# Attention into a softplus layer on one core: ten groups by seven block products instead of eight, a whole k cast with two half-size DMA transposes, 26 fillers, and a new written order

## The chip, the cores and the metric

The kernel runs on one core of one Trainium2 chip. A core has five engines with an instruction queue each: TensorE (PE) for matmuls, VectorE (DVE), ScalarE (ACT), GpSimd (POOL), and SyncE (SP), which here only issues DMAs. Every queue is worked off in order; semaphores make one engine wait for another. Matmuls write to PSUM, which has eight banks of 128 x 512 fp32; DVE and ACT can read PSUM. The metric is the device time of one execution in microseconds (us), lower is better.

## The reference, cut to what matters

```python
scores = scale * q @ k.T                       # 4 sequences, 8 heads, 768 tokens, head size 64
keep   = is_global | is_local                  # the first 8 tokens, and the last 96 up to the query
bias   = -slopes[h] * dist                     # dist = n_local for a global token outside the window
a      = softmax(where(keep, scores + bias, -1e9))
x      = (a @ v).reshape(3072, 512)            # heads side by side
h      = x @ w_in                              # 512 -> 2048
g      = maximum(h, 0) + log1p(exp(-abs(h)))   # softplus
out    = g @ w_out                             # 2048 -> 512, float32
```

Inputs and output are float32; the matmuls of the kernel are bf16.

## The kernel before, in words

The 3072 tokens are 24 blocks of 128. Two neighbouring blocks of a sequence make a unit (12 units, `UNITS`) and, in the order in which they are worked on, a group of 256 tokens (`NGRP` = 12) for the two big matmuls. Each block attends to itself and to the block before it, of which the first 8 keys, outside every window, are replaced by the 8 global ones.

For a unit, q, k and v are loaded as float32 (`load_unit`), cast to bf16 (`cast_q`, `cast_rows`) and q and k transposed, so that the head size lies on the partitions. For units 0 to 2 the transposes are matmuls (`transp_pe`); for units 3 to 11 they are DMA transposes issued from SP (`transp_dma`). `cast_rows` casts k and v in quarters of 64 x 512, because it also swaps halves of tokens between partitions; so a unit takes four k casts and then one transpose of 128 x 1024.

For a block n the steps have names that come back in the order below: `sc` scores (16 matmuls of 128 columns), `z` adds the bias from PSUM to SBUF (DVE), `ex` takes the exponential (ACT), `pv` multiplies by v (8 matmuls of 65 columns per half, the 65th gives the sum), `nm` divides (DVE), and `xt` transposes the result into XT: by matmuls for the first six blocks (with an eviction `xc`), by a DMA transpose from SP for the others. `gk` and `gv` copy the global keys and values. Blocks 0 and 1 get their bias by a matmul (`sb`).

For a group g: `a{g}.{p}` is one of eight pieces of the first matmul (8 matmuls of 256 columns, into one of the two banks h0 and h1), `e` takes its exponential and `ln` the logarithm of 1 + it, which is softplus (ACT). The second matmul is done in two ways. Groups 0 to 3 (`mm2`) take 2 x 16 matmuls of 512 columns into one bank per 128 tokens, then one copy `oc` and one store `st` each. Groups 4 to 11 (`FIRST_S` = 4) use a scheme in the manner of Strassen and Winograd on 2 x 2 blocks: five differences of token blocks (`token_sums`, named `ka`), seven products of eight 256-column matmuls each (`products`, named `b{g}.3`, `.4`, `.5`, `.2`, `.1`, `.7`, `.6`), and additions in the output buffer (`oe{g}.a` to `oe{g}.7`). The sums of weight blocks that this takes (`weight_sums`, 20 operations named `ws`) are made once.

What runs where and in what order is written out: `ORDER` is a list of all operations with the engine of each, in one sequence; each engine's queue is that sequence cut down to the engine. `Program` only checks that nothing stands before what it depends on. The numbers for durations and ranks in the code do nothing at run time. Which PSUM bank an operation uses is fixed by tables (`PE_KEYS`, `PV_KEYS`, `O_KEYS`, `S_KEYS`): from block 4 on `pv` uses the bank x, and products use the bank o except in the last two groups. 35 fillers (`fill`, matmuls on a blank tile into bank x) stand where the order leaves TensorE without work.

Loads of later units are held back by `gates`: each waits for a certain piece `a{g}.{p}` (`LEADS`).

Of the kernel before, what the change touches and what calls it, by code (L numbers as in the profile page):

```python
# [16 lines left out]
class Op:  # L17
    __slots__ = ("name", "eng", "fn", "deps", "sync", "ins")


class Program:


    def __init__(self, placed):
        self.placed = placed
        self.ops, self.writer, self.readers = {}, {}, {}

    def op(self, name, eng, dur, rank, fn, reads=(), writes=(), after=(), dma=None, sync=(), count=1,
           port=False, alts=None, mutex=None):
        o = Op()  # L30
        o.name, o.eng, o.fn, o.sync, o.ins = name, eng, fn, list(sync), None
        if alts:
            o.eng = self.placed[name]
            assert o.eng in alts, (name, o.eng)
            o.fn = lambda: fn(o.eng)
        assert o.eng == self.placed[name], name
# [19 lines left out]
    def in_order(self):  # L56

        done = set()
        for name in self.placed:
            o = self.ops[name]  # L60
            assert all(d.name in done for d in o.deps), (name, [d.name for d in o.deps if d.name not in done])
            done.add(name)
            yield o
        assert len(done) == len(self.ops)
# [4 lines left out]
blank:V ldq0.1:A iota:G ldk0.0:S fill0:P ldq0.0:A ldk0.1:S fill1:P dl0a:V fill2:P table:A ldq1.0:S dl1a:V dl0b:V  # L69
fill3:P dl0c:V ldv0:S fill4:P dl1c:V d0:G ldq1.1:S dl1e:V fill5:P d0e:V fill6:P ldk1.0:S biasTrue4:A biasTrue7:A  # L70
biasTrue0:V fill7:P biasFalse4:G biasTrue6:A biasTrue1:V castq0.1:A ldk1.1:S ones:G castk0.0:A biasFalse5:V ldv1:S
ident:G biasFalse7:A biasFalse2:V biasFalse1:A win0:S castq0.0:A castk0.1:G win1:S biasFalse0:V biasTrue3:A trq0.0:P
biasFalse6:A win3:S biasFalse3:A biasTrue5:A trk0.0:P biasTrue2:V cpq0.1:V fill8:P sb0.0:P cpk0.0:A cpq0.0:V fill9:P
castv0.00:G win2:S cpk0.1:A castq1.0:V castv0.11:A sc0.0:P castv0.01:V fill10:P ldq2.0:S sb1.0:P ex0.0:A castk1.0:G
sc1.0:P win4:S ex0.1:A sb1.1:P castq1.1:G win5:S ex1.0:A pv0.0:P sc1.1:P castv0.10:G nm0.0:V fill11:P fill12:P
ex1.1:A castk1.1:V pv0.1:P trq1.0:P castv1.10:G ldq2.1:S nm0.1:V fill13:P fill14:P cpq1.0:A castv1.11:V pv1.1:P
trk1.0:P nm1.1:V pv1.0:P cin0:G win6:S fill15:P cpk1.1:A cpk1.0:V fill16:P xt0:P cpq1.1:A fill17:P fill18:P
castv1.01:G xc0:A fill19:P win7:S fill20:P nm1.0:V sc2.0:P castv1.00:G cin1:A xt1:P z2.1:V fill21:P gk4:A fill22:P
cin3:G ldk2.0:S gv4.1:A fill23:P z2.0:V sc3.1:P fill24:P xc1:V gv4.0:G sc3.0:P ex2.0:A ldk2.1:S a0.1:P cin2:G z3.1:V
fill25:P a0.0:P e0.1:A z3.0:V castq2.0:G wout0:S ex2.1:A pv2.0:P a0.3:P e0.0:A nm2.0:V ln0.0:A fill26:P cin4:G  # L80
wout1:S fill27:P fill28:P pv2.1:P a0.2:P e0.3:A nm2.1:V ex3.1:A ldv2:S fill29:P cin5:V xt2:P castq2.1:G wout2:S
fill30:P ex3.0:A fill31:P xc2:V a0.5:P e0.2:A pv3.0:P cin6:G wout4:S fill32:P e0.5:A fill33:P nm3.0:V a0.4:P cin7:V
wout3:S pv3.1:P trq2.0:P e0.4:A castk2.0:G nm3.1:V a0.7:P ln0.1:A cpq2.0:V castk2.1:G xt3:P a0.6:P e0.7:A xc3:V
cpq2.1:A cout0:G trk2.0:P e0.6:A ldq3:S a1.1:P cpk2.0:V wout5:S ln0.2:A ws0.6:G wout6:S a1.0:P cpk2.1:V wout7:S
e1.1:A sc4.0:P ws0.4:G e1.0:A a1.3:P ln1.0:A z4.1:V cout1:G a1.2:P castv2.01:A z4.0:V ex4.1:A b1.0.0:P castv2.00:G
fill34:P b1.0.2:P gk5:A ws0.7:V e1.3:A b0.0.0:P b0.0.2:P ex4.0:A cout4:V sc5.0:P castv2.10:V a1.5:P e1.2:A cout3:G
z5.0:V cout2:A pv4.0:P a1.4:P ws0.1:G nm4.0:V ln0.3:A sc5.1:P b0.0.4:P e1.5:A castq3.0:G z5.1:V pv4.1:P castv2.11:A
b0.0.6:P b0.0.8:P cout5:A gv5.1:G ldk3:S nm4.1:V a1.7:P ws0.3:V ln1.1:A xt4:P b0.1.0:P ldv4:S ws2.6:V b0.0.10:P
trq3:S ex5.0:A cout6:V b0.1.2:P b0.1.4:P gv5.0:V e1.4:A b0.1.6:P xc4:V ex5.1:A b1.0.4:P ws2.1:V b0.1.8:P ws2.4:V
ln1.2:A pv5.0:P castk3.01:G b1.0.6:P nm5.0:V b0.1.10:P castk3.00:A a1.6:P castk3.10:V gk6:G ws2.3:V castk3.11:G  # L90
pv5.1:P b1.0.8:P e1.6:A nm5.1:V b0.0.12:P ldq4:S cout7:A b1.0.10:P ws1.3:V ws1.1:G trk3:S b0.1.12:P e1.7:A xt5:P
b0.0.14:P xc5:V b0.1.14:P ws2.7:V oc0.0.0:A a2.1:P ln1.3:A ws1.7:V a2.0:P ldk4:S e2.1:A ws1.4:V b1.0.12:P oc0.1.0:A
castq4.0:G b1.0.14:P ldv3:S e2.0:A a2.3:P ln2.0:A oc1.0.0:V gv8.0:G a2.2:P st1.0.0:S ws1.6:G e2.3:A ldq5:S gv8.1:A
# [59 lines left out]
LOAD_LEAD = 2.5  # L153
LEADS = {3: 2.25, 4: 2.75, 5: 3, 6: 3, 7: 3.5, 8: 3, 9: 3, 10: 3, 11: 2.75}
FILLERS = 35
TABLE_RANK = -9000.0
BIAS0_ON = ["ACT"]
BIASA_ON = ["ACT"]
PE_BIAS = (0, 1)
# [88 lines left out]
def kernel(  # L248
# [116 lines left out]
    def held(keys):  # L365

        return sorted({key[:2] for key in keys})
# [904 lines left out]
```

## Time and profile before

| | |
|---|---|
| time, median of 3 runs | 213.35 us (213.26 to 213.78) |
| span of the profiled execution | 213.6 us |
| PE busy | 202.9 us, 95% |
| ACT busy | 177.8 us, 83% |
| DVE busy | 158.3 us, 74% |
| POOL busy | 107.3 us, 50% |
| moved by DMA | 40.99 MB, mean 192 GB/s |

The profiled execution is one run of its own; its span, from the first to the last instruction, is 0.25 us above the median of the timed runs. Busy PE time is the union of matmuls whose ends are modelled, so overlapping matmuls count once and a busy PE may still be waiting for short moments. In the rows below, a group of instructions has its line, engine, operation, the tile written and the tiles read, shapes, count, busy time, the mean of one in ns, and the idle time of its engine just before. In the rows by stretches each engine has its busy us and, in brackets, its instructions. In the chain of work a row is a start, a duration and what ran.

### The profile page before, as it was taken

How to read it: one execution, taken by the hardware profiler on the slowest of the kernel's cores; microseconds unless marked ns; L12 is line 12 of the kernel's file. 1: busy time of each engine (PE TensorE's matmuls, PEld its weight loads, DVE VectorE, ACT ScalarE, POOL GpSimd, SP SyncE). 2: the span in 40 equal slices, each digit the busy share in tenths (PEclk: the TensorE clock that was granted, in tenths of full speed). 3: DMA queues.
4: the chain of work that ended last, by engine and by line, in shares of the span. 5: the costliest groups of instructions: out<-in, count | busy, mean ns of one | idle time of the engine just before them, and what ended most of it. 6: DMA issues, size and time to landing. Idle time of an engine off the chain costs nothing.

```text
span 213.6 us, 5384 instructions
## 1 busy us (share of the span) xinstructions
PE 202.9 (95%) x2149; PEld 159.8 (75%) x2163; DVE 158.3 (74%) x289; ACT 177.8 (83%) x257; POOL 107.3 (50%) x127
## 2 busy tenths in 40 slices
PE   6699999899999979999999999999999999999994
PEld 1465796556666557776898888988889889888883
DVE  6459577989585978667889869779879857535674
ACT  5787989988998679899998898888997998789410
POOL 4277495542887955751276764627544635003000
PEclk9799999999999999999999999999999999999999
DMA  5999999594999948999679791999759211500205
GB/s 199 326 363 387 387 354 354 203 221 120 302 197 290 147 112 187 274 227 237 198 192 182 193 227 13 186 233 204 183 126 245 77 25 42 142 19 2 98 13 188
DMA packets 69849, 40.99 MB, mean 192 GB/s; under 512 B 30144, under 2 KB 61376, under 8 KB 69824
## 3 DMA queue, kind: packets, MB, share of 16 engines
q1 hardware_dynamic: 69392, 39.99, 72.2%
q10 hardware_dynamic: 432, 0.66, 0.8%
q8 instruction: 17, 0.28, 0.5%
q14 instruction: 8, 0.07, 0.1%
HBM read 27.26 MB, written 6.29 MB: 157 GB/s over the span
## 4 chain that ended last, share of the span: by engine, by line
PE 81%; DVE 7%; issue 4%; ACT 3%; DMA 2%; POOL 1%; ACTq 0%; POOLq 0%; DVEq 0%
PE h_ps L956 37%; PE o_ps L512 18%; PE o_ps L1003 6%; PE s_ps L846 5%; PE x_ps L898 4%; PE s_ps L1003 3%; DMA raw<-in_q_dram 2%; PE x_ps L1116 2%; DVE z L872 2%; ACT e L971 2%; PE x_ps L512 1%; DVE vb L658 1%; PE s_ps L512 1%; PE s_ps L721 1%; DVE xs L910 1%
## 5 line engine op out<-in xcount | busy, mean ns | idle before, releaser
L956 PE MATMUL h_ps<-XT,w_in_bf 128*128 128x256 bf16 x768 | 94.5, 273 | 0.9 <-ACT e L971 0.9
L956 PEld LDWEIGHTS <-w_in_bf 128*128 128x128 bf16 x768 | 72.8, 98 | 12.6 <-issue 1.0
L971 ACT ACTIVATE e<-h_ps 128x512 f32<-128x512 f32 x96 | 59.1, 636 | 11.8 <-PE h_ps L956 11.1
L982 ACT ACTIVATE g<-e 128x1024 bf16<-128x1024 f32 x48 | 49.9, 1052 | 0.8
L872 DVE TENSOR_TENSOR z<-s_ps,biasA 128x1024 f32<-128x1024 f32 x38 | 45.8, 1219 | 5.4 <-PE s_ps L846 2.5
L879 ACT ACTIVATE pb<-z 128x1024 bf16<-128x1024 f32 (+1 forms) x44 | 43.2, 989 | 3.8 <-DVE z L872 3.5
L447 POOL TENSOR_TENSOR raw<-g 128x1024 bf16<-128x1024 bf16 x8 | 17.0, 2130 | 23.3 <-ACT g L982 17.7
L512 PEld LDWEIGHTS <-g 128*128 128x128 bf16 x256 | 24.6, 98 | 2.9
L1003 PE MATMUL o_ps<-w_out_bf,g 128*128 128x512 bf16 x87 | 22.5, 379 | 0.6 <-issue 0.2
L658 POOL CAST kb<-raw 64x512 bf16<-64x512 f32 x24 | 15.6, 652 | 14.1 <-DMA raw<-in_k_dram 9.0
L898 PEld LDWEIGHTS <-pb 128*128 128x128 bf16 x352 | 16.6, 98 | 5.0 <-issue 1.0
L512 PEld LDWEIGHTS <-raw 128*128 128x128 bf16 x192 | 18.4, 98 | 2.0
L1003 PEld LDWEIGHTS <-g 128*128 128x128 bf16 x128 | 11.5, 98 | 10.8
L658 POOL CAST vb<-raw 64x512 bf16<-64x512 f32 x24 | 15.5, 645 | 8.0 <-DMA raw<-in_v_dram 7.2
L909 DVE RECIPROCAL rcp<-x_ps 128x4 f32<-128x4 f32 x40 | 7.2, 180 | 14.8 <-PE x_ps L898 14.6
L910 DVE TENSOR_TENSOR xs<-x_ps,rcp 128x256 bf16<-128x256 f32 x40 | 17.0, 425 | 1.4
L764 POOL COPY vb<-vb 4x512 bf16<-4x512 bf16 x20 | 12.3, 616 | 11.2 <-PE x_ps L898 10.7
L512 PE MATMUL o_ps<-raw,raw 128*128 128x256 bf16 x144 | 17.8, 272 | 0.0
L634 POOL CAST qb<-raw 128x1024 bf16<-128x1024 f32 (+1 forms) x12 | 11.7, 972 | 10.5 <-DMA raw<-in_q_dram 10.4
L898 PE MATMUL x_ps<-vb,pb 128*128 128x65 bf16 x304 | 15.8, 193 | 0.8 <-DVE xs L910 0.8
L512 PE MATMUL o_ps<-raw,g 128*128 128x256 bf16 x128 | 15.9, 273 | 0.0
L447 POOL TENSOR_TENSOR g<-g 128x1024 bf16<-128x1024 bf16 x4 | 8.8, 2204 | 9.1 <-DVE raw L447 8.9
(110 smaller groups left out, 253.0 us busy)
## 6 DMA issues: line engine op xcount, KB each, us to landing
raw<-in_v_dram SPq DMA_DIRECT2D x12, 512.0 KB, 4.8
out_dram<-osb SPq DMA_DIRECT2D x22, 256.0 KB, 2.8
raw<-in_q_dram SPq DMA_DIRECT2D x9, 512.0 KB, 4.4
raw<-in_k_dram SPq DMA_DIRECT2D x9, 512.0 KB, 4.4
raw<-in_moe_w_in_dram SPq DMA_DIRECT2D x8, 512.0 KB, 9.5
raw<-in_moe_w_out_dram SPq DMA_DIRECT2D x8, 512.0 KB, 8.8
raw<-in_k_dram SPq DMA_DIRECT2D x6, 256.0 KB, 6.2
raw<-in_q_dram SPq DMA_DIRECT2D x4, 256.0 KB, 7.5
```

What stands on the lines that cost most here:

```text
L447: (nc.vector if eng == "DVE" else nc.gpsimd).tensor_tensor(dst, a[0], b[0], ALU.subtract)
L512: nc.tensor.matmul(psum(j), lhs[:, f // 2, f % 2, :], w(f), start=(f == 0), stop=(f == 7))
L658: copy_on[eng](dst, src)
L764: copy_on[eng](vb_of(prev)[sl, :, 0:D], vb_of(first)[sl, :, 0:D])
L872: nc.vector.tensor_tensor(z, src, bias, ALU.add)
L879: nc.scalar.activation(pb[:, 0:nr, :].rearrange("p (y a) b -> p y (a b)", y=2), src, AF.Exp, scale=1.0 / root_d)
L898: nc.tensor.matmul(xv[:, h, :], pb[:, 4 * (h % 2) + 2 * part + h // 2 if lone else u_all * (2 * (h % 2) + h // 2) + u, :], vb_of(prev if u ...
L910: nc.vector.tensor_tensor(xs[:, 4 * part : 4 * part + 4, :], xv[:, :, 0:D], rcp[:][:, :, None].to_broadcast([P, 4, D]), ALU.mult,)
L956: last = nc.tensor.matmul(hv[:, j, :], w_in_bf[:, m, fb * P : fb * P + P], XT[g % NXG][:, m, :], start=(m == 0), stop=(m == NM - 1),)
L971: nc.scalar.activation(e[:, p % 2, :, :].rearrange("p j (b t r) -> p (j b) r t", b=2, r=2), hb[:].rearrange("p (a r t) -> p a r t", a=4, r=2),
L982: nc.scalar.activation(gt[:, 2 * p - 2 : 2 * p + 2, :].rearrange("p a t -> p (a t)"), e[:].rearrange("p a j t -> p (a j t)"), AF.Ln, bias=1.0,
L1003: nc.tensor.matmul(bank(key)[:, 0 : z - a], gt[:, fb, ns * P : ns * P + P], w_out_bf[:, fb, a:z], start=(fb == 0), stop=(fb == NFB - 1),)
```

## The change

- `FIRST_S` goes from 4 to 2: groups 2 and 3 also take seven products. `mm2` stays for groups 0 and 1.
- For units 3 to 11, k is cast in one operation of 128 x 1024 (`castk{i}.0`) that regroups heads and token parity along the free dimension, and the swap between partitions that the four quarter casts did is done by the transposes: two DMA transposes of 64 partitions each (`trk{i}.0`, `trk{i}.1`), one per block, instead of one of 128.
- 26 fillers instead of 35.
- The PSUM bank of an operation is written beside it in `ORDER` (`pv0.1:P@h0`); `pv`, products and the early `xt` may now use x or o in turn.
- `ident` is made by a copy from a float32 identity.
- `ORDER` is new throughout: the sequence on every engine, and for many casts, copies and sums also the engine. The load order of the weights and of units 0 to 2 changes with it.

Operations by engine that change most (before, after): v casts on ACT 12, 19, on POOL 24, 16; k casts of units 3 to 11 on POOL 24, 6, on DVE 7, 1, on ACT 5, 2; token sums on DVE 28, 30, on POOL 12, 20; weight sums on DVE 10, 13, on POOL 10, 7; copies of global keys on ACT 10, 1, on POOL 2, 9; evictions of XT on ACT 1, 4, on DVE 5, 2; transposes of k on SP 9, 18.

```diff
-FIRST_S = 4
+FIRST_S = 2
-FILLERS = 35
+FILLERS = 26
...
+        if which == "k" and i not in WIDE:
+            into = tile_.rearrange("p (m r y d) -> p m r y d", m=NPAIR, r=2, y=2)
+            what = raw_t[slot][:].rearrange("p (m y r d) -> p m r y d", m=NPAIR, y=2, r=2)
+            op(f"castk{i}.0", "POOL", lambda eng: copy_on[eng](into, what), reads=raw_keys(slot),
+               writes=[("kb", i % NQB, z) for z in range(4)], port=True, alts=ANY)
+            return
...
-        op(f"tr{which}{i}", "SP", 1.45, rank, lambda: nc.sync.dma_start_transpose(dst, src), dma=(1.24, 18.0),
-           reads=[(which + "b", i % NQB, x) for x in range(4)], writes=keys)
+        for x in range(2):
+
+            def fn(x=x):
+                dst = kt_unit(i)[:, x, :, :].rearrange("p m (r t) -> p (m r) t", r=2)
+                return nc.sync.dma_start_transpose(dst, src[64 * x : 64 * x + 64].rearrange("p a h d -> p (a h d)"))
+
+            op(f"tr{which}{i}.{x}", "SP", fn, dma="trh", reads=[(which + "b", i % NQB, y) for y in range(4)],
+               writes=[kt_tile(i) + (x, r) for r in range(2)])
...
-        xv = bank(key)[:, 0 : 4 * (D + 1)].rearrange("p (h e) -> p h e", e=D + 1)
+        homes[x] = ("x", "o", "h0", "h1") if n < 4 else ("x", "o")
```

The two orders where the prediction speaks of them, the start first:

```diff
-blank:V ldq0.1:A iota:G ldk0.0:S fill0:P ldq0.0:A ldk0.1:S fill1:P dl0a:V fill2:P table:A ldq1.0:S dl1a:V dl0b:V
...
-ident:G biasFalse7:A biasFalse2:V biasFalse1:A win0:S castq0.0:A castk0.1:G win1:S biasFalse0:V biasTrue3:A trq0.0:P
+ldk0.0:S ldq0.0:A blank:V iota:G fill2:P@x ldk0.1:S ldq0.1:A fill18:P@x dl0a:V dl1a:V fill12:P@x ldk1.0:S table:A
...
+biasA2:A fill3:P@x castk0.1:A ident:V fill9:P@x biasF4:G biasA5:A trk0.0:P@s0 castq0.1:A biasF5:G biasF6:A biasF1:A
+trq0.0:P@s1 ones:G biasA6:A biasF3:A castk1.0:A castq1.0:V fill17:P@x biasF2:G cpk0.0:V cpq0.0:A ldq2.0:S cpq0.1:A
```

TensorE's queue from the last `pv` of block 11 to the first piece of group 5:

```diff
-pv11.1 b3.1.0 sc12.0 a4.5 a4.6 b3.1.4 sc13.0 a4.7 pv12.0 b3.1.8 b3.1.12 a5.0
+pv11.1 a4.6 a4.7 b3.3 b3.4 sc13.0 a5.1
```

More of the change, by code (lines that the diff above doesn't have):

```diff
@@ L56, in in_order @@
     def in_order(self):
-        done = set()
+        done, holds, left = set(), {}, {x: len(m) for x, m in self.members.items()}
         for name in self.placed:
@@ L217 @@
[L217 to L240 removed]
+LAST_HOMES = ("x", "o", "s0", "s1", "h0", "h1")
@@ L1137, in attend, with attend_in @@
-    def attend(n, rank):
+        x = f"fill{j}"
+        homes[x] = ("x",)
+        op(x, "PE", lambda: nc.tensor.matmul(x_ps[:], blank[:, 0:P], blank[:]), reads=["blank"], banks=(x,))
+    def attend_in(i):
+        if i in WIDE:
+            for which in "qk":
+                if i not in UNCAST:
+                    cast_q(i, which)
+                transp_pe(i, which)
+        else:
+            for which in "qk":
+                cast_q(i, which)
+                transp_dma(i, which)
+        cast_rows(i, "v")
```

804 lines of the change are left out of this document (352 added, 452 removed).

## The prediction

> **What bounds the kernel now.** I read the head of the page first, then the busy time of each engine by stretches, then the chain of work, then the groups by shape. The head: total busy time by engine, and TensorE's busy tenths in 40 slices.
>
> ```profile
> span 213.6 us, 5384 instructions
> PE 202.9 (95%) x2149; PEld 159.8 (75%) x2163; DVE 158.3 (74%) x289; ACT 177.8 (83%) x257; POOL 107.3 (50%) x127
> PE   6699999899999979999999999999999999999994
> ```
>
> TensorE has work for 202.9 of 213.6 us; only the first slices, one slice near 75 us and the last are short of full. The stretches say how much is idle in each (length, then busy us of PE, PEld, DVE, ACT, POOL, then granted clock, DMA share, GB/s):
>
> ```profile
> core 0: us, PE busy (x) PEld busy (x) DVE busy (x) ACT busy (x) POOL busy (x), PEclk, DMA share, GB/s
> 0.00:8.00 8.00, 4.29 (x22) 1.93 (x23) 3.91 (x17) 5.31 (x13) 3.35 (x12) 0.98 0.73 229
> 20.00:32.00 12.00, 11.90 (x131) 10.02 (x131) 8.32 (x17) 10.48 (x16) 7.91 (x9) 1.00 1.07 372
> 32.00:41.00 9.00, 7.93 (x88) 5.54 (x87) 7.80 (x10) 8.77 (x13) 5.72 (x6) 1.00 0.97 327
> 64.00:77.50 13.50, 11.82 (x119) 7.31 (x119) 11.00 (x17) 9.59 (x15) 10.63 (x16) 1.00 0.94 199
> 77.50:100.00 22.50, 22.34 (x247) 16.63 (x250) 15.49 (x32) 21.49 (x30) 12.64 (x18) 1.00 0.94 220
> 100.00:125.00 25.00, 25.00 (x296) 21.74 (x295) 21.95 (x40) 23.67 (x35) 13.81 (x13) 1.00 0.84 194
> 207.30:213.60 6.30, 3.22 (x30) 2.65 (x27) 2.85 (x6) 0.00 (x0) 0.00 (x0) 1.00 0.46 168
> ```
>
> Idle PE time is 3.71, 0.10, 1.07, 1.68, 0.16, 0 and 3.08 us in these rows, 9.8 of the 10.7 us that the whole run has. So the start, 32 to 41, 64 to 77.5 and the end can give something; from 77.5 on the time is the sum of the matmuls, and every column saved there counts. ACT is the next engine, with 21.49 of 22.5 and 23.67 of 25 us. The end gives nothing: the last product runs to 210.5 and the last store is issued 0.5 us later. The written end of the new order has the same shape (products 1, 6, 7 of the last group last).
>
> ```profile
> 209.49 1.04 PE L512 MATMUL s_ps<-raw,raw 128*128 128x256 bf16 x8
> 211.01 0.35 ACTq L548 DMA_DIRECT2D out_dram<-osb  x1
> ```
>
> **The change part by part.** First, groups 2 and 3 by seven products. The chain of work has ten 512-column matmuls and two products of eight 256-column matmuls back to back:
>
> ```profile
> 43.49 2.16 PE s_ps L1003 x10
> 186.92 1.75 PE o_ps L512 x16
> ```
>
> That is 0.216 and 0.109 us each. Removed: 2 x 32 x 0.216 = 13.8; added: 2 x 56 x 0.109 = 12.2. **-1.6 us on the path.** Its price elsewhere, and that of the moved work, comes from these groups (busy us, mean ns of one):
>
> ```profile
> L1116 PE MATMUL x_ps<-blank 128*128 128x512 bf16 x32 | 11.6, 458 | 1.3 <-DVE blank L1055 1.2
> L447 DVE TENSOR_TENSOR raw<-g 128x1024 bf16<-128x1024 bf16 x16 | 10.9, 688 | 3.0 <-ACT g L982 1.7 <-PE o_ps L512 0.7 <-PE s_ps L512 0.6
> L447 POOL TENSOR_TENSOR raw<-g 128x1024 bf16<-128x1024 bf16 x8 | 17.0, 2130 | 23.3 <-ACT g L982 17.7 <-ACT vb L764 3.4 <-PE o_ps L512 2.1
> L477 DVE TENSOR_TENSOR osb<-osb,o_ps 128x256 f32<-128x256 f32 x6 | 2.5, 422 | 8.2 <-ACT e L971 5.7 <-PE o_ps L512 2.4
> L1032 DVE COPY osb<-o_ps 128x512 f32<-128x512 f32 x4 | 2.8, 689 | 1.2 <-PE o_ps L1003 1.2
> L658 POOL CAST kb<-raw 64x512 bf16<-64x512 f32 x24 | 15.6, 652 | 14.1 <-DMA raw<-in_k_dram 9.0 <-issue 2.9 <-ACT e L971 1.2
> L658 ACT CAST kb<-raw 64x512 bf16<-64x512 f32 x5 | 3.1, 613 | 0.1
> L634 POOL CAST qb<-raw 128x1024 bf16<-128x1024 f32 x9 | 9.8, 1092 | 9.5 <-DMA raw<-in_q_dram 9.4
> L658 ACT CAST vb<-raw 64x512 bf16<-64x512 f32 x12 | 7.4, 616 | 0.2
> L934 ACT COPY XT<-h_ps 128x512 bf16<-128x512 bf16 x1 | 0.6, 603 | 0.0
> L982 ACT ACTIVATE g<-e 128x1024 bf16<-128x1024 f32 x48 | 49.9, 1052 | 0.8
> L616 ACT CAST w_out_bf<-raw 128x1024 bf16<-128x1024 f32 x3 | 3.1, 1039 | 0.0
> ```
>
> The ten added token sums go, net, 2 to DVE and 8 to POOL (30 and 20 against 28 and 12): 1.4 and 17.0 us. The output of such a group takes a copy, two 256-wide subtractions and three 512-wide adds, 4 x 0.69 + 2 x 0.42 = 3.6 us, where two copies took 1.4: +4.4 us for both groups, nearly all DVE. What hides it is DVE's slack (74% busy); without it 4.4 + 1.4 us would stand against the 1.6.
>
> Second, the k cast of units 3 to 11. 36 quarter casts go (24 on POOL at 0.65, twelve on DVE and ACT at 0.61 or less: some 23 us of engine time); nine whole ones come, six of them on POOL, at the q cast's 1.09: 9.8 us. POOL wins 15.6 - 6.6 = 9 us, which about pays half of its token sums. Off the path either way. The nine transposes become eighteen. A q transpose (1024 wide) held the SP queue 1.27 us and the half as large XT transposes 1.22 (median), so size hardly matters:
>
> ```profile
> 72.11 1.27 SPq L741 DMA_TRANSPOSE qT<-qb  x1
> L941 SPq DMA_TRANSPOSE XT<-xs x15: 1189/1225/1715, 66.2 to 164.2; - x15
> DMA to landing us min/median/max: 2.4/4.1/5.9
> ```
>
> So SP gets 9 x 1.2 = 11 us more, spread over some 120 us; queued behind them are loads and the XT transposes, and for these a first matmul waits. The bytes are the same. The Trainium skill, "DMA: Bandwidth & Descriptors", section "Rules for kernel authors", says that two transfers to disjoint partition halves serialize on the same engines and are better made one. That speaks against this part; no run here shows a half transpose yet, and by this rule the split is worth nothing but its issue time, which is already in the 11 us.
>
> Third, fillers: nine fewer, but 13 instead of 8 stand ahead of the first transpose. The clock shows why it matters (length, PE busy, granted clock, DMA), with the first 16 transposes at the start and 8 at full clock:
>
> ```profile
> 4.60:7.10 2.50, 0.00 (x0) 1.00 1.00 287
> 8.00:11.00 3.00, 3.00 (x20) 0.50 1.08 357
> 7.11 1.41 PE s_ps L721 x16
> 27.95 0.45 PE s_ps L721 x8
> ```
>
> PE idles 2.5 us, and then 3.0 us run at half clock: at full clock about 1.5 us less, all in the chain of work. Five more fillers of 0.46 us (mean of the first group above, less when back to back) cover 1 to 2.3 us of that gap. Against it: the new order puts a k cast of unit 1 and four bias operations on ACT between the last q cast and the q evictions that block 0's scores wait for. Ends -1.5 and +1.0; I take -0.5, since the first mm1 also waits for w_in, whose landings are set by a DMA at a share of about 1. The Trainium skill, "TensorE: Matmul & The Clock Gate", Part 1, has the gate judge free-running windows of about 3.4 us; the half clock for 3.0 us agrees in length. By that rule a gap of 1 us no longer halves the clock and the whole 1.5 us would come: a rival below. That fillers fall away elsewhere costs nothing: they ran only where PE had nothing else.
>
> Fourth, the order. In 32 to 41 the loads of unit 2's q and k now stand ahead of four w_in blocks, so its scores can start earlier: between 0 and the 1.07 us of idle PE, I take -0.5. In 64 to 77.5 the 1.68 us come from this:
>
> ```profile
> 68.35 0.41 PE L898 MATMUL x_ps<-vb,pb 128*128 128x65 bf16 x8
> 69.01 0.42 DVE L910 TENSOR_TENSOR xs<-x_ps,rcp 128x256 bf16<-128x256 f32 x1
> 71.75 2.50 POOL L412 TENSOR_TENSOR raw<-raw,raw 128x512 bf16<-128x512 f32 x2
> 71.81 2.72 DVE L658 CAST vb<-raw 64x512 bf16<-64x512 f32 x1
> 75.82 1.06 ACT L879 ACTIVATE pb<-z 128x1024 bf16<-128x1024 f32 x1 [2.96 <-DVE z L872]
> 76.39 0.40 PE L898 MATMUL x_ps<-vb,pb 128*128 128x65 bf16 x8 [0.79 <-DVE xs L910]
> ```
>
> A v cast on DVE lasts 2.72 us while POOL sums weights beside it, block 9's softmax comes late, and PE waits. The new order brings the weight sums forward and gives POOL 7 instead of 10. The same pair can meet again, so between -1.7 and 0; I take -1.0.
>
> What the order makes worse is the lead of XT. From the last pv of a group's second block to the group's first mm1, the written orders hold this much PE work (products 0.87, scores 0.55, pv 0.35): group 3, 4.6 before and 3.6 after; group 5, 6.9 and 3.9; group 6, 6.0 and 3.9; group 8, 5.5 and 4.1; group 9, 7.3 and 5.2. The chain behind it: pv starts at 68.35, xs is ready at 69.43 (1.1), and the transpose lands 4.1 us after its issue (median): 5.2. With the pv itself the new lead in groups 3, 5, 6 and 8 is about 4.3. At the median they would wait 0.9 each, at the shortest landing 0: 0 to +3.6. I take +1.2, a third: group 3 waits today already, and the later landings are the short ones (DMA share down from 0.94 to 0.84).
>
> ACT gets seven more v casts (4.3 us) and three more evictions of XT (1.8), and loses some casts and small copies: at most +6 us on 177.8, hidden as long as ACT stays below PE; rival B prices the place where it may not.
>
> Sum, against the profiled execution: 213.6 - 1.6 - 0.5 - 0.5 - 1.0 + 1.2 = 211.2. The profile's span is 0.25 over the median of the three runs (213.35), so **211.0 us**.
>
> **The rivals.** (A) XT's lead decides, slower. Place: the first mm1 of groups 3, 5, 6 and 8, behind a fuller SP queue. For: today's slacks are small and 11 us more of transposes stand in that queue. Against: from 100 us on nothing waits for XT today. If a landing takes 5.7 us instead of 4.1, a place waits 5.7 + 1.1 - 4.3 = 2.5; with two or three such places, some 6 us, the time is 213.6 - 3.6 + 6 = 216.0. It decides from 0.9 us at each of the four places on, where the 3.6 us of gains are eaten. (B) ACT takes over at the start, no change. For: in 20 to 41 us ACT idles only 1.52 + 0.23 us, and about 2.9 us more of ACT work (three v casts 1.8, three evictions 1.8, one logarithm 1.05, less a w_out cast 1.04 and some 0.7 of small ones) stand ahead of group 2. Against: ACT there waits for PE at times. Then 1.2 us come on top and the two 0.5 do not come: 213.6 - 1.6 - 1.0 + 1.2 + 1.2 = 213.4. (C) All of the start comes, faster: the clock holds (1.5), 32 to 41 and 64 to 77.5 fill up (1.07 + 1.68), XT costs nothing: 213.6 - 1.6 - 4.2 = 207.8.
>
> **How the numbers follow.** The forecast (209.5 to 212.6) 0.43, C 0.14, B 0.12, A 0.31. The measurement tells about 0.3% (0.6 us) from no change. Of B half is within it and a little counts to each side: faster 0.58, same 0.08, slower 0.34. The likeliest is 211.0; the range takes in C and the middle of A, 207.5 to 216.5, and leaves out A's far end and luck below C.
>
> **What would show it.** Matmuls of the 512-column form: 64 instead of 128; products 560 instead of 448, PE busy without fillers down by 1.6. The granted clock between 7 and 11 us at 1.00 (else the 0.5 falls). Idle PE under 1 us around the first scores of blocks 8 and 9. Wrong: idle PE of over 1 us ahead of the first mm1 of groups 3, 5, 6 or 8, released by XT or a DMA (A); ACT without idle from 20 to 50 us and PE waiting for e (B); a DVE busy over 90% with PE waiting for xs, which no rival here prices.

## The result, and the profile after

The changed kernel takes 221.51 us (median of four runs, 219.5 to 221.85), the kernel before 213.31: a ratio of 1.0342, with a 95% interval of 1.0274 to 1.041. The forecast was 211.0 us, its range 207.5 to 216.5. All ratios below are to the kernel before, timed beside it on the same chip, with their 95% intervals. The ratios are of the fast runs alone, the times are medians of all runs, so the two need not divide out exactly.

The head of the page of the changed kernel: span, busy time, TensorE's busy tenths in 40 slices, and the granted clock.

```profile
span 220.0 us, 5485 instructions
PE 202.8 (92%) x2193; PEld 163.0 (74%) x2202; DVE 165.8 (75%) x305; ACT 180.1 (82%) x256; POOL 101.9 (46%) x104
PE   7688999998997979979998999999989999999993
PEclk9999999999999999999999999999999999999999
```

TensorE is as busy as before (202.8 against 202.9 us), though its written work is 1.6 us less and nine fillers are gone. A busy row counts a matmul from start to modelled end (a mean of 273 ns for one of 256 columns, which takes 109 when they run back to back), so every short interruption adds busy time. The Trainium skill, "Trainium Kernel Development and Optimization", section "Best Practices", says not to judge how far a kernel is from the roofline (the best rate that the engine can give) by TensorE's matmul busy share; this trace agrees: the same busy time, and 8.2 us more.

What has to be read is idle time by stage. Cuts are at the first pieces of groups 0, 2, 3, 5 and 11, to some 0.2 us; the two rows on top are the start. Each row: length, then busy us (and instructions) of PE, PEld, DVE, ACT, POOL, then clock, DMA share, GB/s. The changed kernel:

```profile
core 0: us, PE busy (x) PEld busy (x) DVE busy (x) ACT busy (x) POOL busy (x), PEclk, DMA share, GB/s
4.60:7.10 2.50, 2.02 (x14) 0.89 (x12) 0.78 (x3) 2.23 (x6) 2.39 (x7) 1.00 1.05 401
8.00:11.00 3.00, 1.97 (x25) 1.32 (x24) 2.62 (x7) 2.49 (x7) 1.24 (x2) 1.00 1.12 320
...
18.20:51.30 33.10, 31.04 (x315) 21.84 (x319) 27.13 (x49) 31.24 (x46) 16.96 (x19) 1.00 0.94 303
51.30:68.80 17.50, 15.44 (x181) 11.06 (x181) 16.38 (x25) 15.89 (x22) 13.63 (x17) 1.00 1.04 222
68.80:99.40 30.60, 27.01 (x305) 22.53 (x306) 25.78 (x41) 24.96 (x35) 14.93 (x14) 1.00 0.85 191
99.40:193.60 94.20, 92.32 (x1058) 80.19 (x1059) 73.53 (x137) 83.20 (x114) 39.55 (x32) 1.00 0.68 152
```

The kernel before, at the same pieces:

```profile
19.60:51.30 31.70, 30.42 (x301) 21.89 (x303) 26.04 (x44) 27.70 (x40) 18.31 (x20) 1.00 0.89 282
51.30:73.70 22.40, 22.01 (x219) 14.33 (x222) 16.06 (x23) 20.42 (x29) 16.65 (x22) 1.00 1.07 237
73.70:100.40 26.70, 25.10 (x278) 18.71 (x278) 19.63 (x37) 23.54 (x33) 15.17 (x22) 1.00 0.89 209
100.40:188.40 88.00, 87.80 (x1022) 77.05 (x1021) 68.91 (x127) 80.21 (x116) 43.84 (x41) 1.00 0.67 152
```

Idle TensorE goes from 1.28, 0.39, 1.60 and 0.20 us to 2.06, 2.06, 3.59 and 1.88: 6.1 us more, and all stages have a part. (Of the first 2.06, 0.5 lies ahead of group 0's first matmul: 18.2 is its first weight load, the matmul starts at 18.71.)

DVE, 75% busy over the whole run (74% before), is 94% busy in the stage of group 2 (16.38 of 17.5 us; 72% before). Its work there has hardly grown (16.06 us before); the stage has lost the pieces of `mm2` of group 2, which now come later as products. None of the products' sums and additions stands in this stage. Part of its DVE time is copies drawn out beside GpSimd, as two of 4 x 512 values that take 1.78 and 1.37 us, where such a copy by itself takes 0.29:

```profile
52.54 1.78 DVE L704 COPY vb<-vb 4x512 bf16<-4x512 bf16 x1
```

The products' sums and additions of group 2, and the first of group 3, fall into the next stage, 68.8 to 99.4 us, where DVE is 84% busy (25.78 of 30.6 us; 74% before).

The waits of TensorE from the first piece on (what it waited for, us in total, times, longest), first after, then before:

```profile
PE h_ps L903 <- DMA XT<-xs: 1.9, 3, 1.2
PE o_ps L845 <- DVE osb L421: 1.6, 1, 1.6
PE x_ps L845 <- DVE osb L429: 1.1, 1, 1.1
PE h_ps L903 <- DVE z L814: 0.7, 1, 0.7
PE s_ps L788 <- DMA kT<-kb: 0.6, 1, 0.6
PE s_ps L788 <- DMA qT<-qb: 0.5, 1, 0.5
...
PE h_ps L903 <- ACT e L919: 0.3, 1, 0.3
```

```profile
PE s_ps L846 <- DVE z L872: 1.0, 1, 1.0
PE h_ps L956 <- ACT e L971: 0.9, 2, 0.7
PE x_ps L898 <- DVE xs L910: 0.8, 1, 0.8
```

Before, three waits stand out; after, fourteen kinds, most of them once. Besides the one for XT at group 3 (1.2 us) the two longest have plain causes. `pv` of block 11 waits for bank o, which DVE empties late: a token sum stands ahead of that addition, and lasts 3.74 us while GpSimd works without a pause. DVE's and GpSimd's rows:

```profile
90.42 3.74 DVE L379 TENSOR_TENSOR raw<-g 128x1024 bf16<-128x1024 bf16 x1
94.08 0.67 DVE L421 TENSOR_TENSOR osb<-osb,o_ps 128x512 f32<-128x512 f32 x1
```

```profile
89.94 0.60 POOL L704 COPY vb<-vb 4x512 bf16<-4x512 bf16 x1
90.49 1.03 POOL L554 CAST qb<-raw 128x1024 bf16<-128x1024 f32 x1
91.49 2.12 POOL L379 TENSOR_TENSOR g<-g 128x1024 bf16<-128x1024 bf16 x1
```

And `pv` of block 10 waits for bank x behind a copy into the output buffer that group 0's store, written late in SP's queue, had not yet left:

```profile
80.43 0.69 DVE L429 COPY osb<-x_ps 128x512 f32<-128x512 f32 x1 [2.39 <-DMA out_dram<-osb]
```

So two theories at first: L, the lead of XT (rival A); and D, DVE and the banks it empties. Two more came of the runs: S, that the seven products of groups 2 and 3 cause the loss; and O, that the written order runs close behind everywhere, so that no single wait carries the loss.

### The profile page after: what moved, and what is told of

It is laid out like the page before. It is cut to its first block, busy times and chain, and to the rows that moved or that the text cites. A ratio compares the mean times of both kernels' runs of the same rounds, so it can differ in the third digit from the quotient of the medians.

```text
span 220.0 us, 5485 instructions
## 1 busy us (share of the span) xinstructions
PE 202.8 (92%) x2193; PEld 163.0 (74%) x2202; DVE 165.8 (75%) x305; ACT 180.1 (82%) x256; POOL 101.9 (46%) x104
## 4 chain that ended last, share of the span: by engine, by line
PE 48%; DMA 28%; DVE 12%; issue 4%; ACT 3%; SPq 2%; POOL 1%; DVEq 0%; ACTq 0%; POOLq 0%
PE h_ps L903 22%; PE x_ps L442 8%; DMA raw<-in_moe_w_in_dram 7%; PE o_ps L442 7%; DMA raw<-in_v_dram 5%; DMA XT<-xs 5%; DVE z L814 3%; PE s_ps L788 3%; DMA out_dram<-osb 3%; PE s_ps L442 2%; DMA raw<-in_k_dram 2%; DMA kT<-kb 2%; DMA raw<-in_q_dram 2%; PE h_ps L442 2%; DVE vb L704 2%
## 5 line engine op out<-in xcount | busy, mean ns | idle before, releaser
L442 PEld LDWEIGHTS <-g 128*128 128x128 bf16 x320 | 30.6, 98 | 4.1 <-DVE g L379 0.5
L379 POOL TENSOR_TENSOR raw<-g 128x1024 bf16<-128x1024 bf16 x12 | 25.4, 2128 | 7.5 <-PE o_ps L442 3.3
L704 POOL COPY vb<-vb 4x512 bf16<-4x512 bf16 x15 | 10.5, 701 | 29.4 <-PE o_ps L845 25.7
L379 POOL TENSOR_TENSOR g<-g 128x1024 bf16<-128x1024 bf16 x8 | 17.4, 2172 | 8.3 <-DVE raw L379 8.2
L379 DVE TENSOR_TENSOR raw<-g 128x1024 bf16<-128x1024 bf16 x18 | 16.2, 914 | 1.1 <-ACT g L930 0.7
L442 PE MATMUL x_ps<-raw,raw 128*128 128x256 bf16 x128 | 16.3, 273 | 0.0
L545 POOL CAST kb<-raw 128x1024 bf16<-128x1024 f32 x6 | 6.5, 1088 | 13.9 <-DMA raw<-in_k_dram 13.1
L950 PE MATMUL o_ps<-w_out_bf,g 128*128 128x512 bf16 x42 | 12.2, 380 | 0.3
L573 ACT CAST vb<-raw 64x512 bf16<-64x512 f32 x19 | 11.7, 617 | 0.6 <-DMA raw<-in_v_dram 0.2
L845 PE MATMUL x_ps<-vb,pb 128*128 128x65 bf16 x192 | 10.5, 193 | 1.9 <-DVE osb L429 1.1
L857 DVE TENSOR_TENSOR xs<-x_ps,rcp 128x256 bf16<-128x256 f32 x26 | 11.0, 425 | 0.9
L788 PE MATMUL s_ps<-qT,kT 64*128 64x128 bf16 x224 | 9.9, 218 | 1.1 <-DMA kT<-kb 0.6
L442 PE MATMUL o_ps<-raw,raw 128*128 128x256 bf16 x80 | 10.4, 272 | 0.2 <-DVE osb L412 0.2
```

What stands on the lines that cost most here:

```text
L379: (nc.vector if eng == "DVE" else nc.gpsimd).tensor_tensor(dst, a[0], b[0], ALU.subtract)
L442: nc.tensor.matmul(psum(j), lhs[:, f // 2, f % 2, :], w(f), start=(f == 0), stop=(f == 7))
L573: copy_on[eng](dst, src)
L704: copy_on[eng](vb_of(prev)[sl, :, 0:D], vb_of(first)[sl, :, 0:D])
L788: nc.tensor.matmul(reg if unit_of(n) in WIDE else reg.rearrange("p (r t) -> p r t", r=2), kt[rows, 2 * part + m, :], qv(rows, 2 * part + m ...
L845: nc.tensor.matmul(xv[:, h, :], pb[:, 4 * (h % 2) + 2 * part + h // 2 if lone else u_all * (2 * (h % 2) + h // 2) + u, :], vb_of(prev if u ...
```

## The experiments

**Parts of the change alone, in the kernel before.** The k cast and the half transposes:

```diff
-castk3.00 castk3.01 castk3.10 castk3.11 ... trk3:S        (units 3 to 11)
+castk3.0:A ... trk3.0:S trk3.1:S
```

> The kernel before with one part of the change alone: k of units 3 to 11 cast in one operation (on the engines of the changed kernel) and transposed by two half-size DMA transposes. The prediction had this part at no cost for the engines, 9 x 1.2 us more on SP's queue. Theory L1 (the fuller SP queue delays the transposes into XT): XT lands later at several groups and the time goes up by 1.5 to 4 us, 215 to 217. Theory L2 (the written order alone shortens the lead, the half transposes do no harm): within 0.5 of 213.3, or somewhat less.

Measured: 212.87 us, ratio 0.9964 (0.9934 to 0.9994). L1 falls: whatever SP's eighteen transposes delay, the whole cast and the halves together cost no time; the halves alone were not run. Its idle TensorE in the stages of above:

```profile
18.80:49.30 30.50, 30.23 (x298) 21.85 (x302) 24.57 (x43) 28.07 (x40) 16.17 (x18) 1.00 0.96 303
49.30:71.60 22.30, 21.96 (x216) 14.27 (x219) 15.82 (x24) 18.54 (x26) 16.60 (x20) 1.00 1.09 225
71.60:97.30 25.70, 25.00 (x280) 18.76 (x280) 17.42 (x34) 23.45 (x33) 12.47 (x17) 1.00 0.96 208
```

0.27, 0.34 and 0.70 us; the profiled execution of before had 1.28, 0.39 and 1.60. How much of that is the k cast is not told: the next run, with the casts and transposes of before, has 0.91, 0.38 and 1.06 us there.

The fillers:

```diff
-... trq0.0:P ... fill8:P ... fill9:P ... fill12:P        (8 ahead of the first transpose)
+fill8:P fill9:P fill10:P fill11:P fill12:P trq0.0:P       (13)
```

> The kernel before with one edit: five fillers that ran later stand ahead of the first transpose (13 instead of 8). TensorE idled there from 4.6 to 7.1 us and then ran 3.0 us at half clock. The prediction took -0.5 (ends -1.5 and +1.0) for it, the changed kernel's start came 1.4 earlier. If the fillers alone do it: 0.5 to 1.5 less than 213.3, granted clock 1.00 from 7 to 11 us. If landings of q, k and the weights set the pace there: within 0.3 of 213.3, with the clock at 1.00 all the same.

Measured: 213.6 us, 1.000 (0.9963 to 1.0038), with the clock held:

```profile
8.00:11.00 3.00, 2.18 (x31) 1.15 (x32) 1.26 (x4) 2.82 (x6) 1.77 (x3) 1.00 1.10 352
```

Fillers hold the clock; they don't shorten the run by themselves. Both parts together:

> The kernel before with the k cast whole and the half transposes (0.996 of the time before by itself) and with 13 fillers ahead of the first transpose (1.000 by itself, though the first matmul piece came at 17.3 us in its profile instead of 19.6). If the two parts add: 0.994 to 0.998 of the time before, about 212.5 for 213.3. If the earlier start is eaten while the loads land: 0.996.

Measured: 212.21 us, 0.9934 (0.9906 to 0.9963): 0.7% under the kernel before, small but clear of noise. The intervals of this run and of the k cast alone overlap, so how much of it is the fillers' is not told.

**Single waits taken out of the changed kernel.** XT's:

```diff
+        gx = g - 1 if g >= 3 else g
-                        XT[g % NXG][:, m, :],
+                        XT[gx % NXG][:, m, :],
```

> The changed kernel, but from group 3 on the first matmul reads the XT of the group before it, which landed a whole group earlier. So no piece of it can wait for a transpose into XT any more; all other work, transposes too, is unchanged (the output of groups 3 to 11 belongs to other tokens). The changed kernel took 221.5 us, the kernel before 213.3. Theory L (the lead of XT, rival A of the prediction in more places than the four): the pieces wait 1.3 us at group 3 and 0.3 to 0.8 at groups 5, 6 and 9, some 3.0 in all, and what waits behind them is late in turn: 218.5 or less. Theory D (DVE and the PSUM banks: TensorE waits for x and o, which DVE empties late): the waits for XT only hide other waits, the time stays above 220.5. If both were so, between 218.5 and 220.5.

Measured: 220.55 us, 1.0343 (1.03 to 1.0386). Theory L expected 218.5 or less; the ratio is that of the changed kernel. The late stores:

```diff
-      st0.0.0:S behind b2.4, st1.1.0:S behind a3.6, st1.0.0:S behind a4.1
+      st0.0.0:S behind st0.1.0, st1.0.0:S behind trk4.0, st1.1.0:S behind trq5
```

> The changed kernel with three stores of the first two groups written in SP's queue where their rows are ready (the first of group 0 at 51 us instead of 74, those of group 1 at 57 and 66 instead of 79 and 84). Theory D: the copy of products 3 and 4 of group 2 into the output buffer stood 2.4 us behind the store of group 0, and TensorE 1.7 us behind that copy at 80 to 82 us; with the store gone by then 1.5 to 2.0 us come back, 219.5 to 220. Theory L: whatever is won there is lost again at the next XT, within 0.5 of 221.5. A theory of DMA traffic (queues full from 30 to 83 us at a share of about 1) would have the time go up by 0.3 to 1, since three more transfers land among the loads.

Measured: 221.14 us, 1.0373 (1.0322 to 1.0423). The wait for the store is gone from DVE's waits, the time is not. The token sums:

```diff
-ka3.6:G ... ka3.2:G
+ka3.6:V ... ka3.2:V
```

> The changed kernel with two of the token sums of group 3 on VectorE instead of GpSimd. Theory D in the form that DVE and GpSimd cannot work side by side on operands in SBUF: the sum on DVE that took 3.74 us at 90.4 us, three GpSimd operations beside it, takes 0.7 again; the addition behind it that empties bank o comes 3.0 us less two sums of 0.7 earlier, and the 1.7 us that TensorE waits at 93 us fall to 0 to 0.5: 219.8 to 220.3. Theory L: no change, 221.2 to 221.8. If DVE as a whole is too full: slower, 222 or more.

Measured: 220.75 us, 1.0327 (1.0284 to 1.037). The sum that had taken 3.74 us takes 0.68:

```profile
90.23 0.68 DVE L379 TENSOR_TENSOR raw<-g 128x1024 bf16<-128x1024 bf16 x1
```

The mechanism was right, and worth nothing that this measurement can tell. All three edits together:

> The three earlier edits together in the changed kernel: the first matmul of groups 3 to 11 reads the XT of the group before it (output of groups 3 to 11 for other tokens), three stores early, two token sums of group 3 on DVE. Alone they moved the time from 221.5 to 220.6, 221.1 and 220.8. If the waits are few and stand behind one another (each one hidden by the next), the three together give clearly more than the sum of 2.0: 217 or less. If the slack is thin everywhere and every wait removed lets the next one show: 219 to 220.

Measured: 220.87 us, 1.0339 (1.0302 to 1.0376). Not even the sum of the three, and above both ranges. And, on top, scores that read the unit before's q and k:

```diff
+        old = n - 2 if unit_of(n) >= 4 else n
-        qv = q_of(n)
+        qv = q_of(old)
```

> The run with three waits removed (220.9), and one more: from unit 4 on the scores read the q and k of the unit before, which were transposed a unit earlier, so TensorE waits for no transpose of q or k either (output wrong from block 8 on). In the run before it, scores waited for these transposes at 67, 91, 102 and 119 us, 5.0 us in all; no DMA then stands between TensorE and its data from group 3 on. If the loss sits in these arrivals (XT hid them, they hid nothing): 215.5 to 217. If the written order is close behind TensorE on every link, engines too (exponentials, divisions, banks), the next waits show: 218.5 to 220.

Measured: 220.21 us, 1.027 (1.0218 to 1.0321); its interval overlaps that of the changed kernel. From group 3 on TensorE now waits for next to no DMA. Its waits from 50 to 194 us:

```profile
PE x_ps L442 <- POOL raw L379: 1.7, 1, 1.7
PE h_ps L907 <- ACT e L923: 1.2, 3, 0.7
PE x_ps L848 <- DVE vb L573: 0.7, 1, 0.7
PE x_ps L848 <- ACT pb L822: 0.6, 2, 0.4
...
PE h_ps L907 <- DMA XT<-xs: 0.2, 1, 0.2
```

A GpSimd sum, the exponentials, a v cast: other links of the chain. Theories L and D both fall as the cause of the whole; as waits they are real, but the next one stands right behind.

**Where the order changes over.** Every engine's order can be joined at a point: the changed one up to it, the one before from there, or the reverse. The k cast is whole in all, groups 2 and 3 by `mm2`.

```diff
+e5: changed order up to a0.1, then the order before
+e6: changed order up to a2.1, then the order before
+e7: changed order up to a3.1, then the order before
+e8: order before up to a5.0, then the changed order
```

> The written order of the changed kernel up to the first piece of the first matmul (a0.1), and from there the order of the kernel before, with its engines and its PSUM banks; groups 2 and 3 by mm2 as before; k cast whole with half transposes, which alone took 0.9964 of the time before. So of the change only the start and the k cast are in it. In the profile of the changed kernel the first piece came 1.4 us earlier (18.2 against 19.6 us) and the clock held. If that gain stays (the rest of the order before can follow): 0.9964 of the time before less 1.4, 211.2 where the kernel before has 213.3. If the landings of the weights set the pace of group 0 (rival: the gain is eaten in the first group, which took 12.7 us after and 11.0 before): 212.5 to 213.

> As the run before, but the order changes over at the first piece of group 2. In the two profiles this piece starts at the same time, 51.3 us. If the changed order's loss lies behind this point (stages of groups 2 and 4 in the profile: 2.2 and 3.0 us more idle TensorE): 212.5 to 213.5 where the kernel before has 213.3. If the first 51 us leave a hidden debt (softmax, casts and stores later than before, which stage 2 pays): 214.5 or more.

> As the run before, but the order changes over at the first piece of group 3, and there the eight pieces of mm2 of group 2 stand, ahead of it (pv of block 8 in bank x). The changed order lost 2.2 us more than the one before between the first pieces of group 2 and group 3, 1.3 of it as a wait for XT. The pieces of mm2 cover that wait here. Theory L: 213.5 to 214.5 where the kernel before has 213.3 (0.9 of stage 2 stays). Theory D (the stage loses to banks and to DVE, whatever stands ahead of group 3): 215 or more.

> The reverse: the order of the kernel before up to the first piece of group 5 (groups 2 and 3 by mm2), and from there the changed order, with its banks. From this piece on the changed kernel's TensorE idled 2.9 us more than before (8.3 against 5.4), though the work of groups 5 to 11 is the same. If the later order itself is worse (short leads of XT at groups 5, 6, 8 and 9, banks shared by pv and products): 215.5 to 216.5 where the kernel before has 213.3. If the later stages only pay for lateness that came from groups 2 to 4: within 0.7 of 212.9.

Measured: e5 218.03 us, 1.0213 (1.0171 to 1.0255); e6 215.15, 1.0065 (1.0034 to 1.0097); e7 221.5, 1.0357 (1.0302 to 1.0412); e8 222.57, 1.04 (1.0336 to 1.0464).

e6 is the clear one. With the old order from group 2 on, 2.8 of the 3.4% are gone, and the stages behind that point have the small idle times again (0.03 and 0.94 us; 2.06 and 3.59 in the changed kernel):

```profile
50.60:72.10 21.50, 21.47 (x207) 13.87 (x205) 13.16 (x19) 17.37 (x24) 16.15 (x19) 1.00 0.97 226
72.10:98.40 26.30, 25.36 (x281) 18.82 (x278) 17.36 (x34) 23.47 (x33) 12.20 (x16) 1.00 1.00 203
```

By its number (1.0065 of 213.3 is 214.7) e6 just falls into the range of a hidden debt, 214.5 or more. Its profile says otherwise: the first piece of group 2 starts 1.1 us later than in e4 (50.60 against 49.53), and all behind it takes 161.7 us against 162.0. So the loss of this part is there by group 2 and is not paid later; against the k cast alone (0.9964) the first 51 us of the changed order cost 1.0%, where its early start had looked like a gain. What e6 hands back from group 2 on is order and seven products together. The other three fell outside the ranges of both theories; they made waits of their own at the seam, and do not show what they were sent for. In e5 TensorE waits 1.5 us for casts of the weights, which the old order has later than the new start wants them, and 1.8 for scores behind the bias sums. In e7 the copy of group 2's first half waited 3.3 us for a store put at the seam. In e8 the first piece of group 6 waits 3.9 us for XT; the products of group 3 that stand ahead of it in the changed order are missing there.

**The seven products.** Out of the changed order:

```diff
-FIRST_S = 2
+FIRST_S = 4
-b2.3 b2.4 b2.5 ... b3.6, ka2.* ka3.* oe2.* oe3.*
+b2.0.0 ... b2.0.12 ahead of a3.1, the other twelve pieces in the places of products
```

> The changed kernel with groups 2 and 3 by mm2 again: no sums of token blocks, no additions in the output buffer for them, 16 pieces of four 512-column matmuls in place of 14 products; four pieces of group 2 stand ahead of group 3 as cover, the other twelve in the places of products; the three stores early; pv of blocks 8 to 14 in bank x. TensorE has 1.6 us more to do. Theory S (the seven products of groups 2 and 3 cause the loss: all of g must be there before the first, so they cannot cover group 3's XT, their operands and results go through DVE and GpSimd, which hold TensorE up at 80 to 95 us): the 6.0 us more idle of the stages 2 and 4 (2.2, 3.0, and 0.9 of the smaller ones) come back but for 1, less 1.6: 217 to 218.5. Theory O (the order as such, attention close ahead of TensorE everywhere): 221 to 223.

Measured: 224.21 us, 1.0504 (1.0453 to 1.0554). 1.6% more than the changed kernel, of which the 1.6 us of work are 0.7. Theory S expected 217 to 218.5, O 221 to 223: taking the products out does not mend this order, whose places were made for them. Into the order before, both groups:

```diff
-FIRST_S = 4
+FIRST_S = 2
-b2.0.0 b2.0.4 b2.0.8 b2.0.12 b2.1.0 ... b3.1.12
+              b2.3   b2.4    b2.5   ... b3.6           (from the third place on; five weight sums moved up)
```

> The kernel before with groups 2 and 3 by seven products, in its own order: products stand in the places of mm2's pieces from the third on (all of g and 16 weight sums must be ready), the last five weight sums moved up, ten token sums on DVE but one. TensorE has 1.6 us less to do. Theory P (the prediction: -1.6 on the path, the rest hidden by DVE's slack): 211.5 to 212 where the kernel before has 213.3. Theory S (later products uncover XT and the softmax at 64 to 80 us, and DVE's sums and additions stand ahead of softmax): 215 or more, with TensorE waiting at 64 to 80 and 95 to 102 us.

Measured: 231.2 us, 1.0792 (1.0736 to 1.0847). Theory S had the sign; TensorE waits 5.4 us for `pv` banks behind divisions and 4.7 for scores behind the bias sums, both on DVE. And group 3 alone, in the fastest version:

```diff
-b3.0.0 b3.0.4 (ahead of a3.6)  b3.0.8 (ahead of pv10.0)  b3.0.12 ... b3.1.12
+                                                         b3.3 b3.4 b3.5 b3.2, b3.1 behind a5.0, b3.7 b3.6 behind a5.1
```

> The order of the kernel before with the whole k cast, half transposes and 13 early fillers (0.9934 of the time before), and group 3 alone by seven products: TensorE has 0.8 us less to do. All of g must be there before the first product, so the first three pieces of mm2 of this group (2.6 us), which stood between the last pv of block 9 and the first piece of group 4, have no successor there; the written work there falls from 5.1 to 2.5 us, the one short lead in an order that has room elsewhere. Theory P (the prediction's first step): 0.8 less, 0.990 of the time before. Theory L (a lead shorter than pv, division, issue and landing of XT, some 5.2 us, is paid in full where nothing else hides it): TensorE waits 2 to 3 us for XT ahead of group 4; with the 0.8 won, 1.2 to 2.2 us more than without: 0.999 to 1.004 of the time before. If the wait is made up later: 0.992 to 0.996.

Measured: 218.8 us, 1.0278 (1.0231 to 1.0326): by the ratios 3.5% or 7.3 us more than the same kernel without, where 0.8 less were due, and more than theory L priced. From the first piece of group 3 to that of group 6, without the seven products and then with them:

```profile
70.90:83.20 12.30, 12.02 (x147) 9.19 (x142) 8.78 (x16) 11.37 (x16) 7.43 (x11) 1.00 0.85 197
83.20:96.30 13.10, 13.10 (x143) 9.53 (x140) 8.58 (x19) 12.13 (x18) 4.99 (x7) 1.00 0.97 223
96.30:109.90 13.60, 13.60 (x165) 11.88 (x164) 11.09 (x24) 13.45 (x20) 5.13 (x5) 1.00 0.90 229
```

```profile
71.80:84.10 12.30, 10.16 (x135) 8.22 (x131) 8.80 (x17) 11.46 (x16) 6.27 (x9) 1.00 0.96 197
84.10:97.90 13.80, 12.75 (x147) 10.83 (x148) 12.07 (x19) 11.38 (x17) 8.87 (x9) 1.00 1.06 211
97.90:117.30 19.40, 17.02 (x191) 14.31 (x190) 15.09 (x31) 14.00 (x21) 4.88 (x5) 1.00 0.74 164
```

Idle TensorE goes from 0.28 to 5.57 us over the three. In the first, three pieces of `mm2` are missing and the stage is not shorter: what they covered, attention for group 4, takes 12.3 us either way. XT of that group lands 0.1 to 0.2 us ahead of its piece in both; the wait is spread over what stands before the piece, and only 0.2 us of it is shown as one for XT. The last stage also holds three of these products (1, 7 and 6), and there products and additions hand bank o to and fro:

```profile
PE o_ps L509 <- DVE osb L495: 0.8, 1, 0.8
PE o_ps L509 <- DVE osb L478: 0.7, 1, 0.7
```

The places of the products were chosen by hand, and better ones may exist.

**Repairs of the changed order.** Stores early, two sums on DVE, and second halves right behind the first (those of units 3 and 8 stood so already):

```diff
-trk5.0:S ... trk5.1:S        (units 4 to 7 and 9 to 11, 2.5 to 15 us apart)
+trk5.0:S trk5.1:S ...
```

> The changed kernel, whole and with the reference's output, with the repairs that leave its order else alone: the three stores early, two token sums of group 3 on DVE, and the second half transpose of k right behind the first in SP's queue (it was issued 3 to 15 us later, and landed up to 1 us before its scores). If late second halves hold the scores up: 217.5 to 219. If they only hid other waits: 220 to 221.

Measured: 224.97 us, 1.0504 (1.0452 to 1.0556). Slower: TensorE waits 4.5 us for XT and 3.1 for q. The stores and the sums had cost nothing before (e2, e3, e9), so the late second half was worth its place, perhaps because SP works in order and a half that comes too soon holds the transposes behind it; that link was not tested alone. More distance between attention and group work:

```diff
+from a2.1 on, all operations of groups some 8 (e16) or 16 (e17) places later in the one written sequence
+5 (e16) or 19 (e17) operations change between the banks x and o
-LEADS = {3: 2.25, ...}
+LEADS = {3: 2.5, ...}        (e17: {3: 2.75, ...})
```

> The changed kernel with one thing moved: from group 2 on the work of the groups (pieces, products, e, ln, sums, additions, stores) stands about 8 places later in the written order against the work of attention (loads, casts, transposes, scores, softmax, pv, XT), on every engine; the loads are let go a quarter group earlier. TensorE's written work from the last pv to the first piece of a group, 3.6 to 5.7 us in the changed kernel (4.6 to 7.3 before), becomes 4.5 to 6.8. All work and the reference's output stay. Theory T (the order runs too close behind attention on every link, so that single waits removed bring nothing, but distance on all links does): 2 to 4 us less than 221.5, though the shift costs up to 1 us once, at group 2: 217.5 to 219.5. If the distance is not the cause: 221 to 223.

> The same with about 16 places, half a group earlier for the loads: the written work from the last pv to the first piece is 4.5 to 8.8 us. Theory T: another 1 to 2 us less at groups 5 to 11, and 1 more lost once at group 2: 216.5 to 219. If the distance is not the cause, or buffers (four of the exponentials, three of the divided rows) hold attention back when it runs further ahead: 221 or more.

Measured: 241.87 us, 1.1318 (1.129 to 1.1345), and 241.3 us, 1.1302 (1.127 to 1.1334). Twenty us more, and the same for both distances. Of TensorE's waits in the first, those for the banks x and o that DVE or ACT empties add up to some 13 us (3 in the changed kernel). The longest:

```profile
PE x_ps L845 <- DVE osb L429: 2.3, 1, 2.3
...
PE x_ps L845 <- DVE osb L421: 2.0, 2, 1.0
PE x_ps L845 <- DVE osb L426: 1.9, 3, 0.9
PE o_ps L442 <- DVE xs L857: 1.7, 1, 1.7
```

`pv` and products now meet in x and o right after one another, and each waits for DVE to empty the bank for the other. So these runs tell nothing about distance, since the spacing of the banks changed with it.

## Why the prediction was wrong

The forecast, 211.0 us, missed by 10.5 us. Some 2 of them are the base that the sum started from; the other 8.4 are gains that did not come and waits that did. The step that failed is the one by which DVE's slack and the old order's room would hide the price of the change.

**The base of the sum.** It set the span of the profiled execution, 213.6 us, beside the median time, 213.35, and took the difference for 0.25. But a time holds more than a span: 221.81 us with a span of 220.0 in the changed kernel's profiled run, 213.31 with 211.5 in e4's. So the profiled execution of before had taken about 215.5 us, 2 above the median (a later run of the same kernel with a span of 213.6 took 215.54). The same sum, 211.2 us of span, is 213.1 of time: no change instead of faster. Which stretch an ordinary run has shorter is not shown. e11's profile, 212.91 us in the same order but for five fillers, has 3.0 us idle in the four stages where before's had 3.5; its first piece comes 2.3 us earlier.

**"-1.6 us on the path" (seven products).** The work fell, and half of the 512-column pieces is gone; the time did not follow. "What hides it is DVE's slack (74% busy)" was read from the whole run. The sums and additions of the products fall into 68.8 to 99.4 us, where DVE is 84% busy, and four of TensorE's waits there end on them or on the copy that starts the additions: bank o 1.6, bank x 1.1, a token sum 0.3, an addition 0.2, in all 3.2 of 3.59 us idle. And the cover that the pieces of `mm2` had given, which need only a quarter of g each, was counted as nothing: in e18 the stage that lost three of them takes the same 12.3 us, and the whole edit costs 7.3 us on one group in the old order. How much of the changed kernel's loss this step carries is open: e9 took the two longest of these waits away, and the time stayed. The forecast had also named a sign that no rival priced, DVE over 90% busy with TensorE waiting for xs. DVE was so in the stage of group 2, but for work other than the products', and the wait for xs there was 0.4 us.

**Start, -0.5.** The clock was forecast as it came: 1.00 from 7 to 11 us, and in e11 by five fillers alone. The time was not: e11 is 1.000, and the whole changed order up to group 2 costs 1.0% against the k cast alone. The "whole gain" of rival C falls with it. The Trainium skill, "TensorE: Matmul & The Clock Gate", Part 1, has the clock fall after an idle window of some 3.4 us. The changed kernel agrees (no fall, with 0.48 us idle between 4.6 and 7.1 us); in the kernel before 2.5 us idle were enough, and there the measurement decides. The clock is not the bound of the start in either case.

**32 to 41 us, -0.5, and 64 to 77.5 us, -1.0.** Instead, idle time grew: from 1.28 to 1.55 us between the first matmuls of groups 0 and 2, and from 1.99 to 5.65 us from group 2 to 5. The pair that the forecast warned of, a DVE operation beside GpSimd's sums, did meet again (3.74 us for a token sum, 1.78 for a copy).

**XT, +1.2, and rival A.** The waits came, at group 3 (1.2 us) and by the waits view 1.9 us in all, nearer to the forecast than to A. (That group 3 "waits today already" was misread: in the kernel before no wait of TensorE for XT is shown.) A's sign was right, its cause was not: e1 took the wait away and the time stayed. Rival B's extra ACT work came in the first stage (31.24 us busy against 27.70), and the stage is 0.8 us longer from its first matmul on (32.6 against 31.8); but TensorE does not wait for e there, the sign that B named, so B is not shown.

**Half transposes, "off the path either way".** Right, by e4. The Trainium skill, "DMA: Bandwidth & Descriptors", section "Rules for kernel authors", advises one transfer of 128 partitions instead of two halves; here the halves, together with the whole cast, cost no time (0.9964), and no run has them without it.

**As a whole**, an order that is new throughout was priced as a list of edits, each against the slack of the old order, which the new order did not keep; that is theory O, and it is argued, not shown. Shown is that 5.9 us of the loss (2.8%) come with order and seven products from group 2 on (e6), and that the three or four waits taken out do not carry it (e9, e13). What stays open is the share of the seven products and that of the order: each was made for the other, and both mixtures (e10, e12) are slower than either kernel.

## What to carry to other kernels

Before adding up the idle stretches of one profiled execution, find out where that execution stands among its runs: compare times with times. Cover must be read in the stage where the new work falls, on the engine that does it, and what a removed piece of work had covered belongs into the sum. Where an order is rewritten and many short waits appear, taking single ones out tells little; handing the rest of the order back from one point on narrowed the place down in one run (e6), though three other seams (e5, e7, e8) made waits of their own.

## What the runs showed of the hardware that was not expected

A DVE sum of two SBUF operands, 0.68 us by itself, lasted 3.74 us while GpSimd ran three operations in a row, until the last had ended. The Trainium skill, "SBUF — State Buffer", section "SBUF: two separate sides", has DVE and GpSimd share a pair of ports as an exclusive lock for a whole instruction; the trace agrees, and these rows read as if the waiting DVE was passed over each time GpSimd's next operation came at once. That size hardly matters for a transpose was expected, and held: one of 64 partitions held SP's queue 1.19 to 1.32 us in 15 of 18 cases, as long as one of 128.

```profile
56.84 1.24 SPq L673 DMA_TRANSPOSE qT<-qb  x1
58.17 1.23 SPq L680 DMA_TRANSPOSE kT<-kb  x1
```
